# Seven instead of five column blocks of MoE 1 in the first part, with new tile durations in the order's estimate

## The chip, the cores and the metric

The kernel runs on one core of a Trainium2 chip. The metric is the device time of one execution in microseconds (us). Before the change the median of three runs is 1058.14 us (1056.82 to 1059.18).

## The reference

Three layers follow each other; every product is kept at about fp32 precision.

```python
# 1. delta-rule attention: 4 batches x 8 heads, 768 tokens, head width 48
for t in range(768):
    y[t] = q[t] @ state
    state += beta[t] * outer(kn[t], v[t] - kn[t] @ state)
x = y as [3072 tokens, 384]
# 2. MoE 1: one dense layer, d_ff = 2048
h = x @ w_in                       # [3072, 2048]
x = (h * clip(h + 3, 0, 6) / 6) @ w_out
# 3. MoE 2: each token goes to one of 8 experts (argmax of x @ w_gate), 1024 wide
out[token] = gate * (relu(x @ w1[e]) @ w2[e])
```

## The kernel before, in words

**Stages.** The first part runs the attention in chunks of 64 tokens. There are 12 steps `s`, each with two iterations (`it = 2 * s + bp`), and step `s` yields 256 tokens of x. A product in high precision is made of three matmuls, with each operand split into a high and a low tile (names that end in H and L).

MoE 1 has 16 column blocks of 128 of its 2048 columns. The first `NF1` = 5 blocks are computed in the first part, between the attention's work, by `m_stream` (lines 1034 to 1073): for each step, and for each block `f`, nine ph matmuls (x times wi, 256 tokens wide), then ScalarE's t, VectorE's t, ScalarE's gH, GpSimd's gL, and one block later six py matmuls (times wo, 392 columns, in two banks). The t tile has one buffer, ph has two halves, gH and gL have two buffers. At the end of a step the two py banks are copied to yp and written to DRAM as `ypart`. The remaining `NF2 = KF - NF1` = 11 blocks are computed in the second part, in six batches `b` of 512 tokens (lines 1444 to 1490), which then add `ypart`, and choose the expert (`route`). The experts follow (`unit`, `expert_pass`).

**The x tile.** `x_stream` (line 914) transposes an iteration's attention result xr (three matmuls, pX), and writes xTH (ScalarE) and xTL (VectorE). The pair xT of a step has one buffer: for a new step it waits for all ph matmuls of the step before (`need(("Y", s - 1))`) and for the copy of x to DRAM. xr also has one buffer: the output product pO of an iteration waits until the xr of the one before is transposed (`need(("X", it - 1))`, line 887 and after). `chain` is the recurrence itself (pR, pW, pS); pG, pZ, pP and the solve on VectorE (sub, Xp) prepare it.

**Weights.** Block `f` needs two narrowings (`narrow_first`, line 962): a load of 384 KB, one ScalarE and four VectorE instructions, and the splits into high and low. `wi_stream` and `wo_stream` do the blocks of the first part at its start. `ahead_stream` prepares the first `NP` = 3 blocks of the second part near the end of the first; `prepare` (line 1351) does the others during batch 0.

**The order of the first part.** All its streams are generators that yield instructions. `drive` (line 1083) chooses at build time which instruction is emitted next, and each engine runs its instructions in that order. For this, `Clock` keeps an estimate of when each engine and each tile is free. Of the streams whose next instruction could start soonest, with a tolerance of `TOL` times its cost, that with the smallest due time in `DUE` goes first; each "next" that a stream yields takes the next number of its list. `Clock.cost` (line 63) holds the durations of the estimate and `Clock.matmul` (line 130) those at the lower clock. For fp16 matmuls the rule reads:

```python
return max(26 if op.ins[0].free_size() > 64 else 31, n / 2.4 + 2.5) if half else 0.85 * max(n, 128)
```

So a matmul whose stationary operand has 64 columns or fewer counts as at least 31 ns. In pO and pG the operands are split by rows into two halves of 64, in pZ into quarters of 32. The second part and the experts are emitted in program order and not by `drive`.

Of the kernel before, what the change touches and what calls it, by code (L numbers as in the profile page):

```python
# [37 lines left out]
class Clock:  # L38
# [24 lines left out]
    def cost(self, op):  # L63

        n = 1
        for d in (op.ins[0] if "reduce" in op.fn.__name__ else op.out).shape[1:]:
            n *= d
        if "dma" in op.fn.__name__:
            return 40
        half = (op.ins[-1] if op.eng == "pe" else op.out).dtype in (FP16, FP32R, BF16)  # L70
        if op.eng == "pe":
            if op.ins[-1].dtype == FP32R:
                return n / 2.1
            return max(26 if op.ins[0].free_size() > 64 else 31, n / 2.4 + 2.5) if half else 0.85 * max(n, 128)
        fn = op.fn.__name__
        pointers = sum(x.free_size() == 1 for x in op.ins[1:])
        if op.eng == "act":
            return (52 if op.ins[0].space == PSUM else 109) + 95 * (pointers > 0) + 84 * (len(op.outs) > 1) + 0.836 * n
        if op.eng == "dve":
            if half and fn == "tensor_copy":  # L80
                return 64 + 0.26 * n
            if fn == "memset":
                return 60 + (0.38 if half else 0.82) * n
            if fn == "transpose":
                return 70 + 1.06 * n
            if fn == "reciprocal":
                return 70 + 6 * n
            if fn == "tensor_scalar" and op.ins[0].space != PSUM:
                return 66 + 0.52 * n + 60 * (pointers > 0)
            return 70 + (0.52 if all(x.dtype == FP16 for x in op.ins) else 1.04) * n + 60 * (pointers > 0)  # L90
        if op.eng == "pool":
            if fn in ("memset", "tensor_copy"):
                return 80 + 0.81 * n
            wide = op.out.dtype == FP32R or op.out.shape[-1] == 32
            return 60 + (2.5 if wide else 2.15) * n
        raise ValueError(op.eng)
# [33 lines left out]
    def matmul(self, op, t):  # L130

        n, tick = op.out.free_size(), int((t + self.phase) * 3 / 10240)
        rows = op.ins[-1].shape[0]
        half = op.ins[-1].dtype in (FP16, FP32R, BF16)
        while self.tick < tick:
            self.warm = self.columns.get(self.tick, 0.0) >= (3060 if self.warm else 3350)
            self.tick += 1
        self.columns[tick] = self.columns.get(tick, 0.0) + n * (1 if half else 2) * rows / 128
        if self.warm:
            return self.cost(op)  # L140
        return max(27, n / 1.2) if half else 1.7 * max(n, 128)

    def ready(self, tiles):
# [69 lines left out]
def kernel(ctx: ExitStack, tc: tile.TileContext, q, k, v, beta, w_in, w_out, w_gate, w1, w2, out):  # L213
# [13 lines left out]
    CAP = 512  # L227
    YW = DM + E
    RW = DM + E
    NF1 = 5  # L230
    FIRST = 256
    ROWS = [512, 480, 448, 416, 400, 384, 384, 352]

# [33 lines left out]
    half = const.tile([128, 1], FP32, name="half")  # L267
# [83 lines left out]
    with ExitStack() as ax:  # L351
# [594 lines left out]

        wi = [big.tile([128, KD, NF1 * 128], FP32R, name="wi" + x) for x in "HL"]
        wo = [big.tile([128, NF1, YW], FP32R, name="wo" + x) for x in "HL"]

# [26 lines left out]
        def wi_stream():  # L976

            for f in range(NF1):
                yield "next"
# [5 lines left out]
        def wo_stream():  # L985

            for f in range(NF1):
                yield "next"
# [17 lines left out]
        def ahead_stream():  # L1006
# [10 lines left out]
            for f in range(NP):  # L1017
                yield "next"
                for y in weights(NF1 + f, [x[:, :, f * 128:(f + 1) * 128] for x in ahead["wi"]], [x[:, f] for x in ahead["wo"]], Timed(wr, "r", 4),
                                 ("st", 4, "nw", 3, 384, "wt", 2, DM), take, give):  # L1020
# [13 lines left out]
        def m_stream():  # L1034
            for s in range(NS):
# [4 lines left out]
                pend = []  # L1040
                for f in range(NF1 + SKM):
                    if f < NF1:
# [40 lines left out]
        def drive(streams):  # L1083
# [27 lines left out]
            while st:  # L1111
# [4 lines left out]
                if isinstance(x[0], list):  # L1116
                    eng = x[0][0].eng
                    end = t + TOL * sum(clk.cost(o) for o in x[0])
                    same = [y for y in ready if isinstance(y[2][0], list) and y[2][0][0].eng == eng and y[0] <= end]
# [2 lines left out]
                step(x)  # L1122


        TOL = 0.034676
        DUE = [
# [32 lines left out]
        ]  # L1159
        drive([chain(0), chain(1), wc_stream(0), wc_stream(1), o_stream(0), o_stream(1), ql_stream(), qt_stream(), xo_stream(), yo_stream(), kl_stream(), n_stream(), kg_stream(), mx_stream(), kt_stream(), q_stream(), p_stream(), x_stream(),  # L1160
               t_stream(), z_stream(), zero_stream(POOL), zero_stream(DVE)] + [s_stream()]
# [129 lines left out]
    with mx:  # L1291
# [152 lines left out]
        for b in range(NT // 512):  # L1444
# [7 lines left out]
            for f in range(NF2 + SK):  # L1452
# [7 lines left out]
                if f < NF2:  # L1460
                    ph = bank("ph")
                    n = 0
# [167 lines left out]
```

## Time and profile before

| what | value |
|---|---|
| median of three runs | 1058.14 us |
| the profiled execution | 1057.61 us |
| its span, first to last instruction | 1055.9 us |
| PE busy | 897.3 us (85%) |
| VectorE (DVE) busy | 588.3 us (56%) |
| ScalarE (ACT) busy | 561.9 us (53%) |
| GpSimd (POOL) busy | 414.1 us (39%) |
| granted PE clock, mean | 0.929 of full |

The shares are means over three stages with different limits, so the profile is read by stage. A matmul's duration in the profile includes the way through the array; how fast matmuls follow each other is read from the starts in a timeline, or from groups in the chain of waits. Instructions of the first part all stand under line 35, the helper that emits them, and are told apart by their tiles. Idle time is listed with what ended it.

### The profile page before, as it was taken

The numbers are of one execution on the slowest core, as the hardware profiler recorded it, in microseconds if no ns is written. First come the engines' busy times: TensorE is split into PE (matmuls) and PEld (weight loads), VectorE is DVE, ScalarE is ACT, GpSimd is POOL, SyncE is SP. The second block draws the span as 40 slices with busy tenths as digits, with TensorE's granted clock in tenths as the row PEclk, the third lists the DMA queues.
The fourth block names the chain that finished last, engine by engine and source line by source line (L and its number), as shares of the span: only waits on it lengthen the run. The fifth ranks groups of instructions, "written<-read, shape, count | busy, mean of one in ns | idle before, by whom it ended". The sixth has DMA issues, their size and how long they took to land.

```text
span 1055.9 us, 27302 instructions
## 1 busy us (share of the span) xinstructions
PE 897.3 (85%) x11324; PEld 825.2 (78%) x11324; DVE 588.3 (56%) x1500; ACT 561.9 (53%) x1159; POOL 414.1 (39%) x422
## 2 busy tenths in 40 slices
PE   1225788888888788998999999999997999999994
PEld 0224678877787788887888998999896999999993
DVE  6797977969769796646964454453442221122220
ACT  4768767687786767655663323332324442444421
POOL 5353454435434423234421041220105536765731
PEclk9855798989899999998999999999998999999997
DMA  7995988994998857767452223140307435534400
GB/s 172 209 201 103 191 136 148 168 187 91 190 167 180 142 124 153 209 202 220 136 179 92 60 92 106 47 146 6 108 1 277 149 106 156 156 121 135 133 20 19
DMA packets 257669, 143.57 MB, mean 136 GB/s; under 512 B 199875, under 2 KB 240133, under 8 KB 257536
## 3 DMA queue, kind: packets, MB, share of 16 engines
q1 hardware_dynamic: 249712, 123.54, 51.0%
q0 software_dynamic: 7280, 17.41, 5.0%
q8 instruction: 90, 1.47, 0.6%
q10 hardware_dynamic: 544, 0.80, 0.3%
q14 instruction: 43, 0.35, 0.1%
HBM read 76.28 MB, written 35.50 MB: 106 GB/s over the span
## 4 chain that ended last, share of the span: by engine, by line
PE 52%; DVE 17%; ACT 11%; issue 7%; DMA 7%; POOL 4%; SPq 1%; POOLq 0%; ACTq 0%; DVEq 0%
PE ph L1465 12%; PE ph L1256 8%; PE py L1479 4%; PE py L1481 4%; PE py L1480 4%; PE ph L35 4%; DVE Xp L35 3%; PE pz L1244 3%; PE pz L1246 3%; DVE sub L35 3%; PE pz L1245 3%; PE py L35 2%; DVE nw L35 2%; SPq L35 1%; DVE W L35 1%
## 5 line engine op out<-in xcount | busy, mean ns | idle before, releaser
L1260 DVE SCALAR_TENSOR_TENSOR hL<-ph,hH 128x384 fp32r<-128x384 f32 (+6 forms) x64 | 36.1, 564 | 164.1 <-ACT hH L1259 164.1
L1468 ACT ACTIVATE t<-ph,half 128x512 f32<-128x512 f32 x66 | 45.3, 686 | 94.1 <-PE ph L1465 90.6
L1469 DVE SCALAR_TENSOR_TENSOR t<-t,ph 128x512 f32<-128x512 f32 x66 | 45.3, 686 | 85.3 <-ACT t L1468 85.2
L1259 ACT ACTIVATE hH<-ph 128x384 fp32r<-128x384 f32 (+6 forms) x64 | 31.6, 494 | 113.2 <-PE ph L1256 113.2
L35 POOL TENSOR_TENSOR gL<-t,gH 128x256 fp32r<-128x256 f32 x60 | 45.7, 762 | 102.0 <-ACT gH L35 92.8
L1425 POOL DMA_INDIRECT slots<-row,di x24 | 23.9, 996 | 143.6 <-DVE di L1417 138.1
L1473 DVE TENSOR_TENSOR gL<-t,gH 128x512 fp32r<-128x512 f32 x66 | 55.5, 841 | 39.9 <-ACT gH L1472 39.1
L1244 PE MATMUL pz<-a2H,hH 128*128 128x384 f32 (+1 forms) x216 | 73.2, 339 | 0.0
L1246 PE MATMUL pz<-a2H,hL 128*128 128x384 f32 (+1 forms) x216 | 72.4, 335 | 0.0
L1245 PE MATMUL pz<-a2L,hH 128*128 128x384 f32 (+1 forms) x216 | 72.4, 335 | 0.0
L1277 POOL DMA_INDIRECT out_dram<-yo,rw x29 | 28.0, 966 | 110.3 <-ACT yo L1276 106.0
L1472 ACT ACTIVATE gH<-t 128x512 fp32r<-128x512 f32 x66 | 41.6, 631 | 46.3 <-DVE t L1469 46.3
L35 DVE TENSOR_TENSOR Xp<-Xp,sub 128x31 f32<-128x31 f32 (+15 forms) x186 | 64.1, 345 | 3.7
L1256 PE MATMUL ph<-yTL,a1H 128*128 128x384 f32 (+6 forms) x192 | 65.9, 343 | 0.0
L1256 PE MATMUL ph<-yTH,a1L 128*128 128x384 f32 (+6 forms) x192 | 65.9, 343 | 0.0
L1256 PE MATMUL ph<-yTH,a1H 128*128 128x384 f32 (+6 forms) x192 | 65.7, 343 | 0.0
L1479 PE MATMUL py<-woH,gH 128*128 128x392 f32 x192 | 65.5, 341 | 0.0
L1480 PE MATMUL py<-woL,gH 128*128 128x392 f32 x192 | 65.3, 340 | 0.0
L1481 PE MATMUL py<-woH,gL 128*128 128x392 f32 x192 | 65.3, 340 | 0.0
L35 DVE TENSOR_TENSOR sub<-Bt,Xp 128x31 f32<-128x31 f32 (+15 forms) x186 | 62.0, 333 | 4.1 <-POOL Bt L35 0.2
L289 POOL TENSOR_TENSOR a2L<-r,a2H 128x384 fp32r<-128x384 f32 x64 | 62.5, 1007 | 0.0
L35 PE MATMUL ph<-xTH,wiH 128*128 128x256 f32 x180 | 58.7, 326 | 2.9 <-DVE t L35 2.0
(309 smaller groups left out, 3068.3 us busy)
## 6 DMA issues: line engine op xcount, KB each, us to landing
r<-in_moe_w_dram SPq DMA_DIRECT2D x32, 768.0 KB, 4.5
slots<-zrow SPq DMA_DIRECT2D x8, 784.0 KB, 5.9
stage<-in_moe_w_in_dram SPq DMA_DIRECT2D x16, 384.0 KB, 4.1
stage<-in_moe_w_out_dram SPq DMA_DIRECT2D x16, 384.0 KB, 3.9
row<-ypart SPq DMA_DIRECT2D x6, 784.0 KB, 4.5
ysave<-row SPq DMA_DIRECT2D x6, 784.0 KB, 3.6
rw<-slots SPq DMA_DIRECT2D x24, 196.0 KB, 2.9
kr<-in_k_dram SPq DMA_DIRECT2D x24, 192.0 KB, 5.1
```

The lines of the kernel that those rows point to most:

```text
L35: return self.fn(*self.a, **self.k)
L289: in_order(pool.tensor_tensor(dst[1], src_ap, dst[0].bitcast(FP32), ALU.subtract))
L1244: pe.matmul(o, hh[:, ts_], a2[0][:, fp], start=fp == 0, stop=False)
L1245: pe.matmul(o, hh[:, ts_], a2[1][:, fp], start=False, stop=False)
L1246: pe.matmul(o, hl[:, ts_], a2[0][:, fp], start=False, stop=fp == KF2 - 1)
L1256: pe.matmul(ph, a1[a][:, c, fs], xt[x][:, c, 0:n], start=k == 0, stop=k == 3 * KD - 1)
L1465: pe.matmul(ph, wi(a, f)[:, c], xt[x][:, c], start=n == 0, stop=n == 3 * KD - 1)
L1468: act.activation(t_, ph, ACTF.Relu, bias=half, scale=1.0 / 6.0)
L1473: dve.tensor_tensor(gL, t_, gH.bitcast(FP32), ALU.subtract)
L1479: pe.matmul(o, gh[:, ts_], wo(0, fp), start=fp == 0, stop=False)
L1480: pe.matmul(o, gh[:, ts_], wo(1, fp), start=False, stop=False)
L1481: pe.matmul(o, gl[:, ts_], wo(0, fp), start=False, stop=fp == NF2 - 1)
```

## The change

`NF1` goes from 5 to 7, so the second part has nine blocks instead of eleven. Two rules are added to the estimate, for matmuls with a contraction of 64 rows or fewer, at the full and the lower clock. `TOL` and all numbers of `DUE` are replaced; lists of the streams that follow the number of blocks get longer by two blocks. Nothing in the second part's code changes.

```diff
@@ -71,7 +71,9 @@
         if op.eng == "pe":
             if op.ins[-1].dtype == FP32R:
                 return n / 2.1
-            return max(26 if op.ins[0].free_size() > 64 else 31, n / 2.4 + 2.5) if half else 0.85 * max(n, 128)
+            if op.ins[-1].shape[0] <= 64:
+                return max(16 if op.ins[-1].shape[0] == 64 else 12.6, n / 4.8)
+            return max(25.5, n / 2.4 + 2.5) if half else 0.85 * max(n, 128)
@@ -138,6 +140,8 @@
         if self.warm:
             return self.cost(op)
+        if rows <= 64:
+            return max(26.7 if rows == 64 else 21, n / 2.4)
         return max(27, n / 1.2) if half else 1.7 * max(n, 128)
@@ -227,7 +231,7 @@
-    NF1 = 5
+    NF1 = 7
@@ -1122,40 +1126,40 @@
-        TOL = 0.034676
+        TOL = 0.046363
         DUE = [
-            "1244.2 -1574.9 -68.6 -1556.7 207.9 1954.1 -1311.5 -2371.9 3596.5 -5724.5 -1328 1799.8 1726.4",
...
+            "2353.7 -1611.5 -5126.2 -1335.8 -3993.4 -296.7 100.2 -2773 2203.9 -345 3508.9 -1814.7 4967.6",
...
```

## Rows read from the trace of the kernel before

**Rows 1.** Windows view: stretch, length; PE, PEld, DVE, ACT, POOL busy; clock, DMA, GB/s.

```profile
0.00:123.00 123.00, 43.67 (x1016) 38.42 (x1016) 95.81 (x273) 83.81 (x188) 56.78 (x60) 0.70 0.91 172
123.00:402.00 279.00, 233.04 (x5841) 216.34 (x5841) 229.93 (x629) 205.76 (x431) 121.41 (x115) 0.92 0.84 155
402.00:491.00 89.00, 80.25 (x1503) 72.40 (x1497) 49.58 (x119) 55.00 (x119) 31.62 (x35) 0.97 0.69 191
491.00:551.50 60.50, 58.26 (x304) 51.28 (x305) 45.27 (x95) 39.24 (x83) 25.15 (x41) 0.95 0.60 186
551.50:598.30 46.80, 46.80 (x246) 42.39 (x246) 20.18 (x50) 14.64 (x23) 5.63 (x6) 1.00 0.28 86
```

**Rows 2.** Timeline of PE in batch 1: start, duration, instruction.

```profile
568.82 0.39 PE L1465 MATMUL ph<-xH,wiH 128*128 128x512 f32 x1
...
573.00 0.39 PE L1465 MATMUL ph<-xH,wiH 128*128 128x512 f32 x1
```

**Rows 3.** Timeline of GpSimd in batch 0: weight preparation.

```profile
514.35 1.29 POOL L35 TENSOR_TENSOR wiL<-nw,wiH 128x384 fp32r<-128x384 f32 x1 [1.79 <-ACT wiH L35]
...
531.90 1.00 POOL L35 TENSOR_TENSOR wiL<-nw,wiH 128x384 fp32r<-128x384 f32 x1 [2.85 <-ACT wiH L35]
```

**Rows 4.** Timeline of VectorE, the first and the last of step 5's five t tiles.

```profile
300.70 0.42 DVE L35 SCALAR_TENSOR_TENSOR t<-t,ph 128x256 f32<-128x256 f32 x1 [0.60 <-ACT t L35]
...
324.37 0.41 DVE L35 SCALAR_TENSOR_TENSOR t<-t,ph 128x256 f32<-128x256 f32 x1
```

**Rows 5.** Timelines of ScalarE and PE: from step 5 to step 6.

```profile
307.78 0.57 ACT L35 ACTIVATE xr<-pO,qsc 128x384 f32<-128x384 f32 x1
...
322.99 0.28 PE L35 MATMUL ph<-xTH,wiL 128*128 128x256 f32 x1
...
326.91 0.49 PE L35 MATMUL pX<-ident,xr 128*128 128x128 f32 x3
```

**Rows 6.** Timelines of SP and PE in the last batch.

```profile
756.31 0.82 SPq L1216 DMA_DIRECT2D rw<-slots  x2
...
781.96 0.82 PE L1229 MATMUL pxe<-ident,rw 128*128 128x128 f32 x6
```

**Rows 7.** Groups by line, 0 to 490 us: busy us, mean ns, idle before.

```profile
L35 ACT ACTIVATE t<-ph,half 128x256 f32<-128x256 f32 x60 | 28.3, 471 | 30.8 <-PE ph L35 28.9 <-POOL gL L35 1.2 <-issue 0.2
L35 DVE SCALAR_TENSOR_TENSOR t<-t,ph 128x256 f32<-128x256 f32 x60 | 25.0, 416 | 27.1 <-ACT t L35 26.6
L35 ACT ACTIVATE gH<-t 128x256 fp32r<-128x256 f32 x60 | 24.8, 413 | 18.4 <-DVE t L35 17.8
L35 DVE SCALAR_TENSOR_TENSOR nws<-stage,nws 128x384 int32<-128x384 int32 x20 | 11.8, 591 | 0.2
L35 DVE TENSOR_SCALAR nws<-nws 128x384 f32<-128x384 f32 (+1 forms) x20 | 8.5, 428 | 0.9 <-ACT nws L35 0.8
```

**Rows 8.** Chain of waits, 299 and 414 to 428 us: start, us, what.

```profile
299.68 0.88 PE pG L35 x48
...
414.38 0.87 PE pP L35 x24
415.26 0.69 PE pZ L35 x48
...
420.87 1.07 PE ph L35 x9
...
423.05 1.07 PE py L35 x6
424.12 1.63 PE pO L35 x96
...
427.01 0.62 PE pR L35 x24
```

**Rows 9.** Chain of waits, the tail's blocks (step 10).

```profile
460.31 1.34 PE ph L35 x9
...
465.13 1.36 PE ph L35 x9
```

62 rows, old and new, of the table DUE are left out of this document.

## The prediction, made before the change was run

> **What bounds the kernel now.** I read the windows view first, cut at the stages' ends. It shows three machines in one kernel. From 0 to 123 us no engine is full; VectorE is busy 95.8 us of 123 while PE has 43.7. From 123 to 402 us the attention steps run with MoE 1's first part between them: VectorE 229.9 us of 279 (82%), PE 233.0 (84%, at a granted clock of 0.92), ScalarE 205.8 (74%), so several engines are well filled and none is full. From 402 to 491 us VectorE falls to 56% and PE is busy 80.3 us of 89. From 491 us PE is busy without a break in MoE 1's second part (46.8 us of 46.8 in a batch), except in batch 0, which takes 60.5 us. The experts come after the last batch, and the change does not touch them. The numbers stand in [rows 1]. The change takes work out of the stage where PE is the bound, and puts it where the bound is shared.
>
> The next views were timelines of single engines. In the second part one column block starts at 568.82 us and the next at 573.00: 4.18 us, 9 matmuls of 512 columns and 12 of 392 [rows 2]. In batch 0 the weight preparation sets the pace: four wiL subtractions of GpSimd start from 514.35 to 531.90 us, one block in 5.85 us [rows 3].
>
> In the first part the timelines show a loop of MoE 1 with itself. The five t tiles of step 5 start from 300.70 to 324.37 us on VectorE, 5.92 us for a block [rows 4]. The next step's xr had begun at 307.78 us on ScalarE, but its transposes came only at 326.91, after step 5's last ph matmul at 322.99 [rows 5]: x has one buffer, so the attention result waited some 18 us for the blocks. Attention is ahead; the blocks and the hand-over of x are what the next step waits for. This is what speaks most against the change.
>
> **Part 1: the second part loses two of eleven blocks in each of six batches.** Batches 1 to 5 lose 5 x 2 x 4.18 = 41.8 us; PE has nothing else there, so all of it is on the path. Batch 0 prepares six blocks instead of eight and loses between 2 x 4.18 = 8.4 and 2 x 5.85 = 11.7 us; I take 11, because the wiL rows show preparation ending last. Sum: 52.8 us (50 to 53.5). What a shorter batch could uncover has room: in the last batch the first expert's rows are asked for at 756.31 us and wanted by PE at 781.96 [rows 6]; of these 25 us two blocks take 8.4. The first part's partial result is asked for on SP's queue right behind them and wanted by VectorE a little later. If one of them were late, no more than the 8.4 us of that batch would be lost.
>
> **Part 2: weights of two more blocks are prepared before or during step 0.** Each block has two narrowings, each 2 x 591 + 2 x 428 ns on VectorE [rows 7]: 2.04 us, four of them 8.2 us. Ends: 0 us, as VectorE has 27 us free before 123 us and the sixth block is wanted only some 25 us into step 0; 8.2 us, if they stand before the first x tile. I take 3. The four loads of 384 KB are issued by SP in this same stretch, ahead of other loads; what they delay lies within the same ends. ScalarE's and GpSimd's shares of the preparation run on engines less filled there (83.8 and 56.8 us of 123).
>
> **Part 3: 24 more block-steps (two in each of twelve steps) in the first part.** Each costs PE 1.07 us for nine ph and 1.07 us for six py matmuls [rows 8]; VectorE 0.416 and ScalarE 0.471 + 0.413 [rows 7]; GpSimd's gL comes beside, on the engine that is least filled there (121.4 us of 279).
>
> Is there room? I add up PE's need of a step from the chain of waits, where whole groups of matmuls follow each other at the full clock. For one of the 24 iterations: pP 0.87, pZ 0.69, pR 0.62 and as much for pS and each of the two pW (24 matmuls of 48 columns too), pO 1.63, pG 0.88 [rows 8], pX 0.49 [rows 5]: 7.04 us. A step is two iterations and five blocks: 14.1 + 5 x 2.14 = 24.8 us; with seven 29.1. A step from 123 to 402 us lasts 279 / 8 = 34.9 us. So the need would be 83% of it. VectorE goes from 28.7 to 29.6 us of a step, ScalarE from 25.7 to 27.5. Seven blocks fit into today's step; nothing is full, but VectorE stays nearest to it.
>
> Body, eight steps. Ends: if the new order held VectorE at 90% busy, (229.9 + 6.7) / 0.90 = 263 us, 16 us less than now; if PE absorbed nothing, 16 x 2.14 = 34 us more. I take VectorE's row, since it is the fullest of those that feed the loop: 6.7 us of work at 82%, so 8 us more.
>
> Tail, four steps (402 to 491 us): here PE is nearly full. Ends: 8 x 2.14 - 8.75 us of idle time = 8 us; 8 blocks at the pace of the chain there, three ph groups from 460.31 to 465.13 us, so 2.41 us each [rows 9], 19 us. I take 14.
>
> **Part 4: the tile durations in the order's estimate.** The old rule gave 31 ns to every matmul with a stationary tile of 64 or fewer columns: pO 96 x 31 = 2.98 us, pG and pZ 48 x 31 = 1.49 us each. The rows have 1.63, 0.88 and 0.69 us, which is 17, 18 and 14 ns each [rows 8]; the new rule has 16, 16 and 12.6. The old estimate thus saw 2.75 us too much PE work in an iteration, 5.5 in a step, and planned for 24.8 + 5.5 = 30.3 us; the new plan carries 29.1 with seven blocks. That is why I let the body grow by VectorE's work and not by PE's. What the new order itself wins or loses no row shows; its ends are those of the body above.
>
> The rows' 14 to 18 ns are weighed against a page. The Trainium skill, TensorE: Matmul & The Clock Gate, section "Wait — 56ns, not 53.3ns?", says that starts of matmuls never come closer than about 25 ns, however small they are. By that rule pO, pG and pZ would need 192 x 25 ns = 4.8 us, the old durations would be nearer the truth and the seven-block step would need about 32 us of PE. The measured rows decide against it for these row-split tiles, and the sum goes by them.
>
> **Sum.** First part: 3 + 8 + 14 = 25 us more (ends -8 and 61). Second part: 52.8 less. The profiled execution took 1057.61 us, 1.7 more than its span of 1055.9, and lies 0.5 under the median of 1058.14. 1057.6 - 52.8 + 25 = 1029.8; I say 1030.
>
> **Rivals.**
> *The order packs denser.* The body shrinks to the 263 us of the 90% end, the tail gains its small end: 1057.6 - 52.8 - 16 + 8 = 997; half way to the forecast 1013. For it: idle PE time of 46 us in the body, and xr tiles that wait. Against it: five in-order engines, each filled to 74 to 84%, in one loop.
> *The body absorbs half.* 17 us for PE's work there, the high ends of tail and preparation (19 and 8): 1057.6 - 52.8 + 44 = 1049. For it: the pG, pP and pO groups that stand ahead of ph on PE.
> *Slower: the x loop sets the step.* Blocks, hand-over of x, blocks again, with one buffer; then each added block lengthens its step by the pace of a block. At the tail's 2.41 us: 16 x 2.41 + 19 + 3 = 61 us more, 1066; at the body's 5.92 us, 95 + 19 + 3 = 117 more, 1122. It decides from a body growth of 31 us, 1.9 us for each added block. For it: rows 4 and 5, in which the next x waits for the blocks. Against it: of the 5.92 us only about 2.4 are the block's own chain; the rest is waiting behind other work on the same engines, which a new order can shift to attention, since that has the 18 us in hand.
> *It doesn't return what it takes.* Shorter batches uncover a load: at most 8 us, so 1038, inside the forecast's case.
>
> **Chances.** Forecast (1020 to 1040) 0.40; denser (under 1020) 0.25; half absorbed (1040 to 1055.5) 0.16; no change 0.04; x loop 0.15. Faster by over 0.2% (2.1 us, about what a measurement of this kernel tells from none) 0.81, within 0.04, slower 0.15. The range leaves out some 0.03 below, under 1004, and the slower rival above 1056.
>
> **What would show it.** Part 1: batches 1 to 5 of 38.4 us with PE busy throughout, batch 0 near 49.5. Part 2: the first x tile at 123 to 131 us. Part 3: the first part ending near 516 us, VectorE still at about 82% in the body, blocks at 3 to 4 us each. The x loop would show as block paces still above 5 us and steps of over 39 us. The forecast fails if the first part ends after 540 us or before 500.

## The result, and the profile after

The changed kernel takes 1033.36 us (median of four runs, 1030.12 to 1036.32), the kernel before 1058.66 in the same comparison. The ratio is 0.9757 (95% interval 0.9717 to 0.9796): faster by 2.4%, against 1030 us forecast. The profiled execution took 1036.32 us with a span of 1034.5, 21.4 us less than the span before. It is the slowest of the four, whose spans go from 1028.3 to 1034.5 us; by the medians the gain is 25.3 us. So a difference of a few us between two profiled executions shows little by itself.

The windows view of the changed kernel is cut at the places that answer to [rows 1]: the first ph matmul of step 0, that of step 8, the first of the second part, of batch 1, and the last addition of a row. Columns: stretch, length, busy us of PE, weight loads, VectorE, ScalarE, GpSimd (with counts), granted clock, DMA share, GB/s.

```profile
0.00:129.90 129.90, 45.61 (x1025) 40.44 (x1025) 98.04 (x278) 85.81 (x194) 60.30 (x63) 0.99 0.86 170
129.90:414.60 284.70, 258.94 (x6107) 243.20 (x6107) 227.08 (x640) 221.49 (x468) 134.82 (x134) 0.96 0.86 155
414.60:523.20 108.60, 99.12 (x1598) 88.64 (x1594) 59.67 (x150) 62.08 (x135) 37.91 (x52) 0.98 0.55 162
523.20:569.10 45.90, 44.74 (x243) 40.16 (x244) 33.24 (x66) 31.80 (x66) 19.01 (x27) 1.00 0.63 189
569.10:763.00 193.90, 193.90 (x1025) 174.54 (x1024) 97.13 (x231) 61.16 (x98) 40.74 (x40) 1.00 0.28 89
763.00:1034.50 271.50, 247.64 (x1446) 235.09 (x1444) 57.23 (x138) 103.42 (x224) 138.83 (x131) 0.96 0.39 124
```

Stage by stage, against the same cuts of the kernel before (123.0, 402.4, 490.9, 551.5, 786.9, 1055.9 us), whose rows from the body on are:

```profile
123.00:402.40 279.40, 233.44 (x5859) 216.71 (x5857) 230.33 (x630) 206.16 (x431) 121.41 (x115) 0.92 0.84 155
402.40:490.90 88.50, 79.75 (x1479) 71.93 (x1474) 49.08 (x118) 54.50 (x118) 31.62 (x35) 0.97 0.69 191
490.90:551.50 60.60, 58.36 (x304) 51.38 (x305) 45.37 (x95) 39.34 (x83) 25.15 (x41) 0.95 0.60 186
551.50:786.90 235.40, 235.40 (x1233) 212.76 (x1233) 110.42 (x251) 74.49 (x118) 40.24 (x40) 1.00 0.23 74
786.90:1055.90 269.00, 246.70 (x1446) 233.98 (x1445) 57.25 (x138) 103.58 (x224) 138.86 (x131) 0.96 0.39 125
```

```
stage                   before   after   change   forecast
to the first ph          123.0   129.9     +6.9      +3
body, steps 0 to 7       279.4   284.7     +5.3      +8
tail, steps 8 to 11       88.5   108.6    +20.1     +14
batch 0                   60.6    45.9    -14.7     -11
batches 1 to 5           235.4   193.9    -41.5     -41.8
experts                  269.0   271.5     +2.5       0
sum                     1055.9  1034.5    -21.4     -27.8
```

In the body PE's busy share rose from 84 to 91% and its granted clock from 0.92 to 0.96, while VectorE went from 82 to 80% (230.3 us of work before, 227.1 after). The two blocks more per step fit in: the pace of a block fell, as VectorE's t tiles of step 5 show, seven of them from 312.79 to 338.30 us, 4.25 us for a block where [rows 4] had 5.92.

```profile
312.79 0.42 DVE L35 SCALAR_TENSOR_TENSOR t<-t,ph 128x256 f32<-128x256 f32 x1
...
338.30 0.42 DVE L35 SCALAR_TENSOR_TENSOR t<-t,ph 128x256 f32<-128x256 f32 x1
```

The second part runs as [rows 2 and 3] said: on PE's timeline a block starts 4.23 us after the one before, and in batch 0 the last four wiL subtractions of GpSimd, which start from 530.75 to 548.51 us, come 5.92 us apart on the mean.

```profile
586.50 0.40 PE L1469 MATMUL ph<-xH,wiH 128*128 128x512 f32 x1
...
590.73 0.39 PE L1469 MATMUL ph<-xH,wiH 128*128 128x512 f32 x1
```

```profile
530.75 1.16 POOL L35 TENSOR_TENSOR wiL<-nw,wiH 128x384 fp32r<-128x384 f32 x1 [2.09 <-ACT wiH L35]
...
548.51 1.30 POOL L35 TENSOR_TENSOR wiL<-nw,wiH 128x384 fp32r<-128x384 f32 x1 [1.79 <-ACT wiH L35]
```

Of the slack that [rows 6] showed, 17.4 us are left: SP asks for the first expert's rows at 740.65 us, and PE's first transpose of them starts at 758.02 without a wait.

```profile
740.65 0.82 SPq L1220 DMA_DIRECT2D rw<-slots  x2
...
758.02 0.82 PE L1233 MATMUL pxe<-ident,rw 128*128 128x128 f32 x6
```

### The profile page after: what moved, and what is told of

Its sections match the earlier page's. It is cut to its first block, busy times and chain, and to the rows that moved or that the text cites. A ratio compares the mean times of both kernels' runs of the same rounds, so it can differ in the third digit from the quotient of the medians.

```text
span 1034.5 us, 27589 instructions
## 1 busy us (share of the span) xinstructions
PE 890.0 (86%) x11432; PEld 822.1 (79%) x11432; DVE 572.4 (55%) x1500; ACT 565.8 (55%) x1183; POOL 431.6 (42%) x446
## 4 chain that ended last, share of the span: by engine, by line
PE 61%; DVE 11%; DMA 9%; issue 7%; ACT 6%; POOL 4%; SPq 1%; POOLq 0%; ACTq 0%; DVEq 0%
PE ph L1469 10%; PE ph L1260 9%; PE ph L35 6%; PE py L35 5%; PE py L1485 4%; PE py L1483 4%; PE py L1484 3%; PE pO L35 3%; PE pz L1248 3%; PE pz L1249 3%; PE pz L1250 3%; DMA KG<-Kbd 2%; DVE nw L35 2%; DMA kr<-in_k_dram 2%; DMA mx<-in_v_dram 1%
## 5 line engine op out<-in xcount | busy, mean ns | idle before, releaser
L35 POOL TENSOR_TENSOR gL<-t,gH 128x256 fp32r<-128x256 f32 x84 | 63.6, 757 | 123.6 <-ACT gH L35 112.7
L35 PE MATMUL ph<-xTH,wiH 128*128 128x256 f32 x252 | 77.1, 306 | 5.1 <-DVE t L35 4.2
L1472 ACT ACTIVATE t<-ph,half 128x512 f32<-128x512 f32 x54 | 37.1, 687 | 71.8 <-PE ph L1469 66.9
L35 PE MATMUL ph<-xTL,wiH 128*128 128x256 f32 x252 | 72.5, 288 | 1.7 <-DVE xTL L35 1.7
L35 PE MATMUL ph<-xTH,wiL 128*128 128x256 f32 x252 | 72.2, 287 | 0.5 <-issue 0.5
L1473 DVE SCALAR_TENSOR_TENSOR t<-t,ph 128x512 f32<-128x512 f32 x54 | 37.0, 686 | 61.9 <-ACT t L1472 55.3
L1477 DVE TENSOR_TENSOR gL<-t,gH 128x512 fp32r<-128x512 f32 x54 | 46.9, 868 | 31.9 <-ACT gH L1476 31.8
L35 ACT ACTIVATE t<-ph,half 128x256 f32<-128x256 f32 x84 | 39.7, 472 | 44.8 <-PE ph L35 38.3
```

The costliest lines, as they stand in the source:

```text
L35: return self.fn(*self.a, **self.k)
L1472: act.activation(t_, ph, ACTF.Relu, bias=half, scale=1.0 / 6.0)
L1473: dve.scalar_tensor_tensor(t_, t_, 1.0, ph, ALU.min, ALU.mult)
L1477: dve.tensor_tensor(gL, t_, gH.bitcast(FP32), ALU.subtract)
```

## The experiments

Theory 1 is that of the prediction: the first part has room for most of the blocks' work, if its order is found for them with the right tile durations. The first rival is the x loop: each block lengthens its step by its pace. The second is that the new order is the gain, and the moved blocks add nothing. All the kernels keep the second part's code. The stages of their profiled executions, with the cuts of the table above (the last column has the medians of the timed runs; beside them the kernel before took 1056 to 1059 us). Each row of stages is one execution; up to step 0 the changed kernel, e1, e5 and e12 run the same order, and their starts lie 2 us apart.

```
kernel                              to 1st ph   body   tail  first part  median
before                                  123.0  279.4   88.5       490.9  1058.7
changed                                 129.9  284.7  108.6       523.2  1033.4
e1  its blocks 5, 6 not issued          129.7  281.1  100.2       511.0  1022.6
e5  their matmuls alone issued          127.9  280.9  105.0       513.8  1800.4
e2  seven, old order                    132.1  330.6  116.3       579.0  1097.0
e3  seven, new durations, old dues      127.0  314.8  107.9       549.8  1065.8
e7  seven, old durations, searched      129.7  305.1  110.6       545.4  1056.8
e9  seven, new durations, searched      134.9  295.1  108.3       538.3  1050.4
e11 changed, searched on                127.1  286.1  108.3       521.5  1030.9
e12 changed, two t buffers              128.0  284.6  107.5       520.1  1033.1
e4  five, order of the change           120.7  280.3   97.2       498.2  1066.1
e6  five, new durations, searched       127.8  257.3   99.6       484.7  1051.6
e8  five, two x tiles, searched         120.4  275.5  103.8       499.7  1065.1
e10 six, new durations, searched        122.9  283.5  102.0       508.4  1051.0
```

**e1: the added block-steps left out, the order kept.**

```diff
-            self.pin(op)
+            if not getattr(op, "off", False):
+                self.pin(op)
...
+                        o.off = left and f in (5, 6)
... # in m_stream, for ph, t, t, gH, gL and py; left is True
```

> The changed kernel with its order kept to the instruction; blocks 5 and 6 of MoE 1 are planned, but none of their 24 steps' matmuls, activations and subtractions is issued (their share of the output is left out; their weights are still prepared). Theory 1 (the first part has room, so a block-step costs less than PE's 2.14 us on the mean): against the changed kernel's first part of 523 us this one ends 15 to 35 us earlier, body (first ph of step 0 to first ph of step 8) shorter by 0 to 15 us, tail by 10 to 20. Rival (x loop: each block lengthens its step by the block's pace): earlier by 16 x 4.3 + 8 x 2.8 = 91 us, body by 69, tail by 22.

The first part ended 12.2 us earlier, the body 3.6 us shorter, the tail 8.4, and the whole took 1022.58 us, 11 less. The rival's 91 us are far off: 24 block-steps cost this order 0.5 us each. The sum is a little under theory 1's range of 15 to 35, and the tail under its 10 to 20. One reason stands in the windows of body and tail: without the blocks the granted clock is 0.91 and 0.90 instead of 0.96 and 0.98.

```profile
129.70:410.80 281.10, 234.52 (x5867) 218.37 (x5867) 223.17 (x625) 208.48 (x436) 122.83 (x118) 0.91 0.87 160
410.80:511.00 100.20, 87.01 (x1474) 76.50 (x1473) 54.88 (x140) 55.87 (x119) 32.17 (x44) 0.90 0.56 170
```

At 2.14 us each, 51 us of matmuls are gone, but PE's busy time in the first part fell only from 403.7 to 365.2 us. What remains runs slower: in the groups by line, from 130 to 409 us, a ph matmul of the same shape takes 311 ns on the mean here, and 287 ns in e5, where the blocks' matmuls are issued (289 in the changed kernel).

```profile
L35 PE MATMUL ph<-xTL,wiH 128*128 128x256 f32 x120 | 37.3, 311 | 2.1 <-DVE xTL L35 2.1
```

```profile
L35 PE MATMUL ph<-xTL,wiH 128*128 128x256 f32 x165 | 47.4, 287 | 0.8 <-DVE xTL L35 0.5 <-issue 0.3
```

The other reason is that the place was filled by other waits. In the waits view (PE, 130 to 411 us: total, times, longest) PE waited 13.6 us for the transposed keys, in the changed kernel 6.2; these are the rows of e1 and of the changed kernel.

```profile
PE pG L35 <- DMA KG<-Kbd: 13.6, 9, 4.6
```

```profile
PE pG L35 <- DMA KG<-Kbd: 6.2, 2, 4.1
```

And the x tile did not come sooner by much. In e1 ScalarE's xr of step 5 starts at 279.41 us and PE transposes it at 299.96; in the changed kernel at 280.96 and 304.88. With two blocks fewer before it, the attention result still waits 20 us for its turn in PE's order. As that order is kept, e1 does not tell what another order could win with x in hand sooner.

```profile
279.41 0.58 ACT L35 ACTIVATE xr<-pO,qsc 128x384 f32<-128x384 f32 x1
...
299.96 0.49 PE L35 MATMUL pX<-ident,xr 128*128 128x128 f32 x3
```

**e5: only the matmuls of these block-steps.** gH and gL are replaced by a weight tile as the operand of py, so the blocks' values are missing from x. Tokens are then routed otherwise, and what follows the first part isn't comparable: the experts alone take 1042 us.

```diff
+                        if left and f in (5, 6):
+                            if o.eng != "pe":
+                                o.off = True
+                            elif o.ins[-1].name.startswith("wo"):
+                                o.a = (o.a[0], wi[0][:, 0, 0:128], o.a[2])
... # the rest as in e1
```

> The changed kernel with its order kept; of the 24 added block-steps all matmuls are issued (the py matmuls take a weight tile in the place of gH and gL, so the values of these blocks are left out), but not the two ScalarE, the VectorE and the GpSimd instruction. The run without the blocks had a first part of 511 us at a granted clock of 0.91 in the body, the changed kernel 523 at 0.96. If PE's matmuls are the price of the blocks: first part 519 to 525 us. If the chain through ScalarE, VectorE and GpSimd is the price: 507 to 513 us, and the clock still at 0.95 or more in the body. If the blocks' matmuls pay for themselves by the clock, it could even end before 507.

513.8 us, with a clock of 0.96 in the body and 0.98 in the tail. Of the 12.2 us between no blocks and all of them, 2.8 fall to the matmuls and 9.4 to the instructions of ScalarE, VectorE and GpSimd; counted from step 0 on, which begins 1.8 us earlier here than in e1, 4.6 and 7.4. With such differences between single executions the split holds only roughly. It lies just over the second answer (507 to 513), and which of the three engines makes the price isn't told apart. From step 0 on PE is busy 33.5 us longer than in e1 and idle 28.9 us less. So of the 51 us of extra matmuls some 29 were taken from idle time; some 18, by the difference of 51 and 33.5, came back as the others ran faster.

```profile
127.90:408.80 280.90, 257.44 (x6106) 243.12 (x6106) 222.52 (x624) 210.24 (x437) 123.06 (x118) 0.96 0.85 157
408.80:513.80 105.00, 97.59 (x1602) 88.43 (x1594) 55.85 (x142) 56.33 (x119) 32.29 (x44) 0.98 0.58 168
```

**e2 and e3: seven blocks without the new due times.**

```diff
-    NF1 = 5
+    NF1 = 7          # e2: all else as before; e3: also the new rules in Clock.cost and Clock.matmul
```

> The kernel before with seven blocks and nothing else: old tile durations, old tolerance and due times (the lists of the streams that got longer keep their last number). Theory 1 with the order's part in it (room alone is not enough, the order must be found for seven blocks): first part over 540 us, whole over 1050 us. Rival (the number of blocks makes the gain, any order gives it): first part near 523 us, whole 1030 to 1040 us.

> Seven blocks and the corrected tile durations with the old tolerance and due times. If the durations carry the gain of the order: 1033 to 1045 us, first part 523 to 535. If the due times carry it: near the run with the old durations, over 1050 us. Theory 1 expects in between, about 1045.

e2 took 1096.97 us, a ratio of 1.0405 (1.0356 to 1.0455) to the kernel before: slower, though the second part returned its full 56 us. Its body takes 330.6 us, and no engine is better used: VectorE is busy 70%, PE's clock is 0.91. Room is not enough; the same blocks cost 88 us in this order. The corrected durations alone bring 29 us of the first part back (e3: 549.8, 1065.79 us, above the expected 1045), the due times with their tolerance another 27.

```profile
132.10:462.70 330.60, 272.48 (x6002) 255.07 (x5998) 232.19 (x633) 218.91 (x458) 133.86 (x133) 0.91 0.68 130
```

**e7 and e9: both estimates searched.** New due times from a random search by the estimate's own end of the first part: e7 with the old durations (5900 trials from the change's due times), e9 with the new ones (3900 trials from the old due times).

```diff
-        TOL = 0.034676
-        DUE = [ ... ]
+        TOL, DUE = ...          # found by the search; NF1 = 7 in both
```

> Seven blocks with the old durations and an order searched by that estimate (5900 trials). If the durations matter by themselves: first part over 540 us, whole over 1050. If any searched order would do: 523 to 535 us and 1033 to 1045.

> Seven blocks, the new durations, and an order searched from the due times of the kernel before (3900 trials): the partner of the searched run with the old durations, whose first part took 545 us. If the corrected durations are worth something to a search: first part 525 to 540 us, whole 1036 to 1050. If only the search counts: within 4 us of that run, 541 to 550 and 1053 to 1060.

1056.75 against 1050.37 us (just over the 1050 expected of e9), first parts of 545.4 and 538.3. The corrected durations seem worth some 7 us to a short search, less than unsearched; as the two searches differ in start and length, that isn't settled. From e9 to the changed kernel there are 15 us more that belong to its own due times; how many trials these took isn't known.

**e4 and e6: five blocks with a new order.**

```diff
-    NF1 = 7
+    NF1 = 5          # e4: the change's due times; e6: searched for five, 6400 trials
```

> The changed kernel with five blocks: new durations, tolerance and due times. Rival (the better order gives the gain by itself): 1030 to 1040 us, with a first part near 465 us. Theory 1 (the moved blocks give it): 1048 to 1062 us, first part 480 to 495 us, second part as before.

> Five blocks with the new durations and an order searched for five blocks by the estimate itself (6400 trials from the changed kernel's due times). Theory 1 (moving the blocks is worth something of its own): first part 472 to 488 us, whole 1038 to 1054. Rival (the better order is all of the gain): first part under 470 us, whole 1036 or less.

e4 took 1066.12 us, somewhat more than expected (1048 to 1062): an order found for seven does not suit five. e6 took 1051.57 us (ratio 0.9953, 0.9927 to 0.9978). A searched order with the right durations gains about 0.5% with five blocks, the change 2.4%. That does not refute the second rival. e9, with seven blocks and 3900 trials from the old due times, ends at 1050.37 us, and e10 below, with six and 4800, at 1051.02: in searches of some thousand trials five, six and seven blocks come out alike. What is shown is that with the due times of the change seven blocks take 1033 us and five 1066. Whether five blocks would also come near 1033 with a search like that behind the change, whose first part is 15 us shorter than e9's, was not run.

e6 also shows a fuller price of the blocks: its first part is 38.5 us shorter than that of the changed kernel, 27.4 of them in the body. The 12 us of e1 are what the blocks cost in an order made for them; I take the rest to be what this order gave up for them, which no run shows by itself.

```profile
127.80:385.10 257.30, 222.68 (x5597) 208.71 (x5594) 205.30 (x572) 200.85 (x418) 121.37 (x115) 0.92 0.92 163
385.10:484.70 99.60, 85.59 (x1646) 78.07 (x1642) 62.03 (x161) 57.84 (x122) 30.56 (x35) 0.95 0.62 171
```

**e8: two x tiles.** `NXT = 2` in e6's place, with an order of its own (4900 trials).

```diff
-        NXT = 1
+        NXT = 2
```

> As the five-block order that was searched, with two buffers for the x tile and an order searched for that (4900 trials). Rival (x loop: the single x tile sets the step): first part at least 15 us shorter than that of the five-block run with one x tile. Theory 1 (shared engines set it): within 8 us of that run.

The first part took 499.7 us, 15 longer than with one x tile: neither the rival's 15 shorter nor theory 1's 8 us either way. The buffer did take away the wait for x. The first xr of step 5 is transposed 2.1 us after it is done, 13.5 us ahead of step 4's last ph matmul, and yet step 5's first ph starts 7 us after that one.

```profile
270.91 0.58 ACT L35 ACTIVATE xr<-pO,qsc 128x384 f32<-128x384 f32 x1 [0.24 <-PE pO L35]
...
273.57 0.53 PE L35 MATMUL pX<-ident,xr 128*128 128x128 f32 x3
...
287.03 0.28 PE L35 MATMUL ph<-xTH,wiL 128*128 128x256 f32 x1
294.14 0.28 PE L35 MATMUL ph<-xTH,wiH 128*128 128x256 f32 x1
```

So x in hand earlier did not shorten the step here, which speaks against the x loop. It is not decisive: the order comes from another search, which may be why the first part got longer, and no order was run with one and with two x tiles.

**e10: six blocks.** `NF1 = 6`, searched (4800 trials).

> Six blocks, new durations, order searched for six (4800 trials). The sixth and seventh block each take some 27 us from the second part. If each block costs the first part about the same (from 485 us with five searched to 523 with seven): first part 500 to 508 us, whole 1036 to 1045. If the seventh costs clearly more than the sixth: under 497 us, whole under 1033, and six would be the better number.

The first part ended at 508.4 us, just over the end of what was expected (508), but the whole took 1051.02 us, a miss: the expectation was set from the changed kernel, and from e6 it would have been 1051.6 + 23.7 for the first part - 26.1 for the second. The sixth block earned nothing over e6. Six against seven isn't settled by this, as the due times of the change come from another search.

**e11 and e12: further on from the changed kernel.** e11 searches its due times on. e12 keeps its order and gives the t tile of the first part two buffers.

```diff
-        t = pool.tile(shape, dt, tag=tag, name=name, bufs=bufs)
+        t = pool.tile(shape, dt, tag=tag, name=name, bufs=2 if tag == "t" else bufs)     # e12
```

> The changed kernel with its order searched on by the same estimate (6200 trials, from its own due times), which takes little more from the estimate (3 us). Expected: first part 514 to 526 us, whole 1026 to 1036. It shows also how far two orders that the estimate holds equal differ on the chip; over 8 us either way would mean that the estimate does not rank such orders.

> The changed kernel, its order the same instruction by instruction, with two buffers for the t tile of the first part instead of one. The chain of a block through ScalarE, VectorE and GpSimd cost 9 us when the matmuls stayed. If the single t buffer makes that price (a block's t waits for the gL before): first part 4 to 9 us shorter, 514 to 519 us, whole 1024 to 1030. If the price is the engines' time, which the buffer doesn't change (ScalarE waited for gL three times, 3.6 us): 520 to 525 us, whole 1030 to 1036.

1030.91 us (ratio to before 0.9752, 0.9719 to 0.9785) and 1033.08 us (0.9796, 0.9771 to 0.9821). Neither differs from the changed kernel (0.9757) by more than the intervals. In e12 ScalarE's waits for gL fell from 3.6 to 2.0 us, and the first part from 523.2 to 520.1; 1.9 of these 3.1 us lie ahead of step 0, where no t tile is written yet. So the single t buffer is not what makes the price that e5 left to ScalarE, VectorE and GpSimd. That it is these engines' time is what remains, and isn't shown by itself. The rows are of the changed kernel and of e12.

```profile
ACT t L35 <- POOL gL L35: 3.6, 3, 1.7
```

```profile
ACT t L35 <- POOL gL L35: 2.0, 2, 1.0
```

## Why the prediction was right

The direction and its reason held: the second part gave back more than the first part took. That the time came so near to 1030 us is partly luck. The first part took 32.3 us instead of 25, the experts 2.5 instead of none, and the second part gave back 56.2 instead of 52.8. And what the new order itself would be worth stood on no row: with due times or durations other than the change's, seven blocks took 1050 to 1097 us (e9, e7, e3, e2), all outside 1020 to 1040; only the search that went on from the change's own (e11) came out like it.

*Part 1* held: 41.5 us in batches 1 to 5 (41.8 forecast), 14.7 in batch 0 (11, upper end 11.7). The sum of 56.2 is over the stated 50 to 53.5. Batch 0 was undersized: its first wiL subtractions start at 523.84 us, 0.6 us after the batch; in the kernel before they start at 494.81, 3.9 us after it.

*Part 2* was 6.9 us, not 3, within its ends. Why it is more isn't shown. Three of the four added narrowings stand ahead of step 0, 5.5 us of VectorE's work, but its busy time there grew by only 2.2 us, so other work moved behind. The order moves this start too: with five blocks step 0 begins at 120.4 to 127.8 us (e8, e4, e6), with seven at 127.0 to 134.9.

*Part 3.* The body grew by 5.3 us (8 forecast), but the working behind the 8 did not hold as stated. VectorE was to get 6.7 us more work at an unchanged 82%; its work in the body fell by 3.2 us, to 80%, as the order moved some of it into the tail (10.6 us more there, of which the added t tiles are 3.3). What does agree is that the blocks' price lies more with ScalarE, VectorE and GpSimd than with PE (e5). What the sum lacked is the clock: I had counted PE's work at the full clock and taken the idle time as the room, but part of the room was that matmuls run faster once the blocks fill the gaps. The tail grew by 20.1 us, just over its upper end of 19. Only 8.4 of these are the blocks (e1). The new orders with five blocks leave 97.2 to 103.8 us for the tail (e4, e6, e8) instead of 88.5, so they put more at the end, whether or not blocks are added. I had split body and tail as if the order could not move work between them; their sum, 25.4, was forecast as 22.

*Part 4* held in kind. The durations of 14 to 18 ns in [rows 8] are worth 29 us of first part at unchanged due times (e2 to e3), and perhaps 7 when both are searched (e7 to e9). In the trace of the kernel before, the 64-row matmuls of pO start in pairs, 2 to 4 ns apart with mostly 28 or 29 ns to the next pair, which makes 17 ns for one in [rows 8]; the 128-row matmuls of pR start 25 to 26 ns apart. The rule of the Trainium skill that was weighed there (TensorE: Matmul & The Clock Gate, section "Wait — 56ns, not 53.3ns?") fits pR and not these row-split tiles. The same page of the Trainium skill, in "Part 3: Packing small matmuls — row/col tiling", says that matmuls on different tiles of the array can run concurrently, which agrees with the pairs.

*The rivals.* The slower one named a price that the old order does have. Seven blocks in it cost 88 us more in the first part and end at 1097 us, inside the 1066 to 1122 that I gave it; the body grows by 51.2 us, over the 31 from which the rival was to decide. With the new order it grows by 5.3, its steps last 35.6 us and a block of step 5 takes 4.25, so there the rival is wrong by its own signs. What sets the steps of the old order with seven blocks wasn't tested: it was not run with two x tiles. That new durations and due times take 56 us off the first part with the one x tile kept (e2 to the changed kernel) says that the single buffer alone does not fix the price. xr waits long before its transposes, in [rows 5] as after the change. I read that as the bound; but without the blocks' work the wait stays (e1), and with two x tiles it goes and the first part gets no shorter (e8). The denser order (0.25) did not come, nor did the half-absorbed body.

The experts' 2.5 us may not be all chance. In the kernels with seven whole blocks this stage, whose code is unchanged, takes 269.7 to 271.6 us from the start of the last addition, with five or six blocks 268.0 to 269.7. Whether the shorter second part costs it some 2 us, and by what, isn't shown.

## What to carry to other kernels

Work moved from a full engine's stage into one with shared idle time can lose if the order there stays as it was. The same move was 4% slower with the old order and 2.4% faster with the new one, while a new order alone, from a search of 6400 trials, gave 0.5%. When orders are searched, compare variants at equal search: in searches of 3900 to 6400 trials five, six and seven blocks came out alike. To price filler work, leave it out of the order that has it, and then put back one engine's part: that told 3 to 5 us of matmuls from 7 to 9 us of the rest. A tile that waits long for its turn is not yet a loop that sets the pace; take the buffer or the work away and see whether the step gets shorter.

## What the runs showed of the hardware

More matmuls can make the others faster. With only the blocks' matmuls put back (e1 to e5), the granted clock rose from 0.91 to 0.96 in the body and from 0.90 to 0.98 in the tail, a ph matmul of the same shape went from 311 to 287 ns, and 51 us of matmuls more gave 35.2 us more of busy PE and 2.8 us more of time. In the sparse start, where PE is busy about a third of the time, the granted clock says little about time: with the same PE order it reads 0.98 in e1 and 0.71 in e5, and step 0 begins at 129.7 and 127.9 us.

```profile
0.00:129.70 129.70, 43.65 (x1025) 38.75 (x1025) 97.61 (x278) 85.89 (x194) 60.09 (x63) 0.98 0.85 170
```

```profile
0.00:127.90 127.90, 45.38 (x1024) 40.29 (x1025) 97.56 (x278) 85.94 (x193) 60.33 (x63) 0.71 0.90 173
```
